# Weight operands prepared one step earlier, and two tiles placed elsewhere in memory, in a fused attention and two-MoE kernel

## The chip, the cores and the metric

The kernel runs on one core of a Trainium2 chip. The metric is device time in microseconds (us), the median of several executions. Before the change it was 1088.23 us over three runs (1085.76 to 1088.39).

## What is computed

Three layers follow each other. The first is linear attention with exponential features (4 batches, 8 heads, 576 positions); the second is a soft mixture of experts with 32 slots; the third, in which the change lies, is a dense mixture of 8 experts over 2304 tokens of width 512, hidden width 1024, with weights P that come from a gate by eight rounds of row and column normalisation:

```
logits = x @ w_gate
P = np.exp(logits - logits.max())
for _ in range(8):
    P /= P.sum(1, keepdims=True) + 1e-09
    P /= P.sum(0, keepdims=True) + 1e-09
    P *= N / E
for e in range(E):
    h = np.maximum(x @ w1[e], 0.0)
    out += P[:, e:e + 1] * (h @ w2[e])
```

All of it is float32 in and out.

## The kernel before

The last layer takes some 800 of the 1084 us. Its input x is the product of a coefficient matrix (2304 x 32) and the 32 slot outputs, so `x @ w1[e]` is made as a product of rank 32. Each float32 operand is split into two parts, high and low, and stacked, so that a single pass over 128 rows gives the exact product. For expert e, `make_stack` multiplies slot outputs with w1 (tile `ps`), VectorE (DVE) splits the result into the second half of the tile `st`, `spread_stack` spreads it over the partitions (matmuls `pr`, weights `rep`), and ScalarE (ACT) writes both halves of `st`. The coefficients stand in five tiles `ct0` to `ct4`; `ct0` to `ct3` hold two blocks of 256 tokens each, `ct4` one.

A block is 256 tokens of one expert; there are 9 to an expert, 72 in all. In a block, `first_layer` issues 8 matmuls `z<-ct,st` (stationary operand: 128 columns of `st`; moving operand: 256 columns of `ct`). `hidden` applies relu and forms the operands of a Strassen-Winograd product with seven products in place of eight: ACT writes each operand's high part (`hh_a` from z directly, `hh_s` from a sum s), DVE or GpSimd (POOL) the low part (`hl_a` on DVE, `hl_s` on POOL: four per block), DVE the sums s. `product(i, k)` then multiplies operand k of block i with the matching operand of w2: 4 chunks by 3 matmuls (high by high, high by low, low by high), 12 of them, into a sum named x, y or z. `take` adds the sum, times P, to the output tile `xo` on DVE. The order of the products k = 0 to 6 is a11, a12, s2, s1, s3, s4, a22, with the weight operands b11, b21, t2, t1, t3, b22, t4; t1 to t4 are differences or sums of quarters of w2.

The weight operands of the next expert are prepared while this one runs. `w_sum(e, n)` makes t1, t2, t3, t4 (n = 0 to 3) on POOL; t4 is made in the place of b21. `w_part(e, k)` makes operand k: ACT writes its high part (a CAST of 128x1024), then POOL its low part (a TENSOR_TENSOR of 128x1024). In the profile b11, b21 and b22 all read `w_b`, t1 to t4 read `w_t`, and a sum's line has `moe_w` or `t` as its output. They go into ten buffers in turn, so that operand k >= 3 of expert e+1 takes the place of operand k-3 of expert e.

The order of the work is written out by hand and kept on each engine. In the main loop, after each product (block `blk`, step `k`), one piece of `hidden` for the next block is issued, then what the tables `W_SUMS` and `W_PARTS` have under `(blk, k)`; a key of 9 stands for block 0 of the expert that is being prepared. `first_layer` of the next block is issued behind the product of k = 2, so between two first layers run the products s1, s3, s4, a22 of one block and a11, a12, s2 of the next. During expert 0, `SINK` also issues pieces of the gate's normalisation, mainly three at k = 1 and two at k = 5; these are small DVE instructions on P and on row and column sums (`rs`, `cs`).

Tiles are laid out one behind the other in pools. `rd_held` takes 16 bytes of a partition, rounded up to 32, and `gst`, the gate's tile, 32. So before the change `ct4` starts at byte 32032 (32 past a multiple of 256) and `st` at byte 190240 (also 32 past). `ct0` to `ct3` and `rep` start at multiples of 256. The `hh` and `hl` tiles stand 96 past a multiple of 256, the weight operands 32 past.

Of the kernel before, what the change touches and what calls it, by code (L numbers as in the profile page):

```python
# [8 lines left out]
F32R = mybir.dt.float32r  # L9
# [9 lines left out]
E, SPE, FF = 8, 4, 1024  # L19
# [34 lines left out]
def tile_kernel(ctx: ExitStack, tc: tile.TileContext, a):  # L54
# [3 lines left out]
    const = ctx.enter_context(tc.tile_pool(name="const", bufs=1, side="left"))  # L58
# [8 lines left out]
    def load_const(name, shape, pool=None, q=SP):  # L67
        t = (pool or const).tile(shape, F32, name=name, bufs=1)
        q.dma_start(out=t, in_=a[name])
        return t  # L70
# [9 lines left out]
    def w1_unit(name, e, n):  # L80
        return unit_t[name, e, n].rearrange("p (k f) -> p k f", k=2)
# [21 lines left out]
    def load_k(t):  # L103
        x = kp.tile([128, 512], F32, tag="kt", name=f"kt{t}")
        SP.dma_start(out=x, in_=a["kT"][t])
        kt_t[t] = x

    def load_v(i):
        x = kp.tile([128, 512], F32, tag="vt", name=f"vt{i}", bufs=3)
        SP.dma_start(out=x, in_=a["vb"][i])  # L110
        vt_t[i] = x
# [287 lines left out]
    load_k(1)  # L399
    load_v(0)  # L400
    load_k(2)
    ident = load_const("ident", [128, 128])
    ones = load_const("ones", [128, 128])
    sel_e = load_const("sel_e", [128, 4], kp)
# [113 lines left out]
    mp = mp_cm.__enter__()  # L518

    ct = [const.tile([128, 512], F32R, tag=f"x{i}", name=f"ct{i}", bufs=1) for i in range(4)]  # L520
    ct.append(const.tile([128, 256], F32R, name="ct4", bufs=1))
    rep = [const.tile([128, 4, 128], F32R, tag=f"x{4 + i}", name=f"rep{i}", bufs=1) for i in range(2)]
    for i in range(2):
        G.dma_start(out=rep[i], in_=a["rep"][:, i * 512:(i + 1) * 512].rearrange("p (g c) -> p g c", g=4))
# [99 lines left out]
    def w_sum(e, n):  # L624


        w = wsrc[e]
        if n == 0:
            G.tensor_tensor(out=w["t1"], in0=w["t3"], in1=w["b11"], op=ALU.subtract)
        elif n == 1:  # L630
            G.tensor_tensor(out=w["t2"], in0=w["t1"], in1=w["b22"], op=ALU.subtract)
        elif n == 2:
            G.tensor_tensor(out=w["t3"], in0=w["t3"], in1=w["b22"], op=ALU.subtract)
        else:
            G.tensor_tensor(out=w["t4"], in0=w["t4"], in1=w["t2"], op=ALU.add)

    def w_part(e, k):

        name = PRODUCTS[k][1]
        s = wsrc[e][name]  # L640
        n = (7 * e + k) % NW
        w = (cl1 if n < 4 else cl2).tile([128, 2, KH, 256], F32R, tag=f"wo{n}", name=f"w{e}_{name}", bufs=1)
        A.copy(out=w[:, 0], in_=s)
        G.tensor_tensor(out=w[:, 1], in0=s, in1=w[:, 0].bitcast(F32), op=ALU.subtract)
        wop[e, k] = w
        if k == 6:
            wsrc.pop(e)
            for n in range(2):
                unit_t.pop(("moe2_w2", e, n))
# [70 lines left out]
    cp = ctx.enter_context(tc.tile_pool(name="cp", bufs=1, side="right", reuse_waits="tile"))  # L720
    pz = ctx.enter_context(tc.tile_pool(name="pz", bufs=1, space=PSUM, reuse_waits="tile"))
    pm = ctx.enter_context(tc.tile_pool(name="pm", bufs=4, space=PSUM, reuse_waits="tile"))
    xo = cp.tile([128, NT, DM], F32, name="xo")
    P = cp.tile([128, NT, E], F32, name="P")

    def acc_tile(name):
        return pm.tile([128, 512], F32, tag="m", name=name)

    def z_tile(n, name):
        return pz.tile([128, 1024], F32, tag=f"z{n}", name=name)  # L730

    def make_stack(e):

        ps = z_tile(0, f"ps{e}")[:, 0:256]
        for kc in range(KC):
            w = w1_unit("moe2_w1", e, kc // 2)
            for g in range(4):
                PE.matmul(ps[32 * g:32 * g + 32, :], sot[:, kc, 0:NS], w[:, kc % 2, g * 256:(g + 1) * 256], start=kc == 0, stop=kc == KC - 1)
        for n in range(2):
            unit_t.pop(("moe2_w1", e, n))  # L740

        st = cp.tile([128, FF], F32R, tag="st", name=f"st{e}", bufs=1)
        hl = st[:, FF // 2:].rearrange("p (n f) -> p n f", n=2)
        V.tensor_copy(out=hl[:, 0, :], in_=ps)
        V.tensor_tensor(out=hl[:, 1, :], in0=ps, in1=hl[:, 0, :].bitcast(F32), op=ALU.subtract)
        return st
# [11 lines left out]
    def sinkhorn():  # L758
# [11 lines left out]
        yield  # L770
        Pf = P.rearrange("p t e -> p (t e)")
        V.tensor_copy(out=Pf, in_=pl[:, 0:NT * E])
# [11 lines left out]
        V.tensor_scalar_sub(Pf, Pf, gm)  # L784
        A.activation(out=P, in_=P, func=AF.Exp)
        yield
        for it in range(8):
            rs = cp.tile([128, NT, 1], F32, tag="rs", name=f"rs{it}")
            V.tensor_reduce(out=rs, in_=P, axis=AX.X, op=ALU.add)
            V.tensor_scalar_add(rs, rs, 1e-9)  # L790
            V.reciprocal(out=rs, in_=rs)
            yield
            V.tensor_tensor(out=P, in0=P, in1=rs.to_broadcast([128, NT, E]), op=ALU.mult)
            yield
            cs = cp.tile([128, 1, E], F32, tag="cs", name=f"cs{it}")
            csf = cs.rearrange("p o e -> p (o e)")
            V.tensor_reduce(out=csf, in_=P.rearrange("p t e -> p e t"), axis=AX.X, op=ALU.add)
            yield
# [4 lines left out]
            yield  # L803
            V.tensor_tensor(out=P, in0=P, in1=cs.to_broadcast([128, NT, E]), op=ALU.mult)
            yield
# [116 lines left out]
    sink = sinkhorn()  # L922
    next(sink)
    stacks = {0: make_stack(0)}
    for k in (4, 5, 6):
        w_part(0, k)
# [7 lines left out]
        pass  # L934
    load_munits(4)

    W_SUMS = {(3, 1): 0, (3, 6): 1, (5, 6): 2, (7, 6): 3}
    W_PARTS = {(2, 6): 0, (4, 6): 2, (6, 6): 1, (8, 1): 3, (8, 6): 4, (9, 0): 5, (9, 1): 6}
    SINK = {1: 3, 5: 2}
    making = iter(())  # L940
    for i, (e, blk) in enumerate(blocks):
# [3 lines left out]
        for k in range(7):  # L945
            product(i, k)
            take(i, k)
            if k == 0 and blk == NBLK - 1 and more:
                stacks[e + 1] = make_stack(e + 1)
            if k == 1 and blk == NBLK - 1 and more:  # L950
                spread_stack(stacks[e + 1], e + 1)
            if k == 2 and i + 1 < len(blocks):
                first_layer(i + 1, 1)
                first_layer(i + 1, 0)
                making = hidden(i + 1)
            next(making, None)
            if more and (blk, k) in W_SUMS:
                w_sum(e + 1, W_SUMS[blk, k])
            if more and (blk, k) in W_PARTS:
                w_part(e + 1, W_PARTS[blk, k])  # L960
            if e and (blk + 9, k) in W_PARTS:
                w_part(e, W_PARTS[blk + 9, k])
            if e == 0:
                for _ in range(SINK.get(k, 0) - (blk == 0 and k == 1)):
                    next(sink, None)
            if i == NBLK - 1 and k in (3, 4):
                scale_row(k - 3)
            if e == 1 and k in (0, 1) and blk + 1 < NBLK:
                scale_row(2 * (blk + 1) + k)
# [66 lines left out]
```

## Time and profile before

| | |
|---|---|
| median of three runs | 1088.23 us (1085.76 to 1088.39) |
| profiled execution, whole | 1086.3 us |
| its span, first to last instruction | 1084.1 us |
| TensorE matmul (PE) busy | 1052.2 us, 97% |
| TensorE weight load (PEld) busy | 982.0 us, 91% |
| VectorE (DVE) busy | 732.0 us, 68% |
| GpSimd (POOL) busy | 687.3 us, 63% |
| ScalarE (ACT) busy | 569.8 us, 53% |

Busy time of PE counts a matmul from its start to its end, and the ends overlap: a matmul over 256 columns shows about 0.28 us, while the next one starts 0.113 us later. So a wait of PE shows as a longer distance between starts before it shows as idle time, and distances between starts are the safer measure. Within the main loop every line of the profile is put down to one helper's line (L50); instructions are told apart by their tiles.

### The profile page before, as it was taken

How to read it: one execution, taken by the hardware profiler on the slowest of the kernel's cores; microseconds unless marked ns; L12 is line 12 of the kernel's file. 1: busy time of each engine (PE TensorE's matmuls, PEld its weight loads, DVE VectorE, ACT ScalarE, POOL GpSimd, SP SyncE). 2: the span in 40 equal slices, each digit the busy share in tenths (PEclk: the TensorE clock that was granted, in tenths of full speed). 3: DMA queues.
4: the chain of work that ended last, by engine and by line, in shares of the span. 5: the costliest groups of instructions: out<-in, count | busy, mean ns of one | idle time of the engine just before them, and what ended most of it. 6: DMA issues, size and time to landing. Idle time of an engine off the chain costs nothing.

```text
span 1084.1 us, 23152 instructions
## 1 busy us (share of the span) xinstructions
PE 1052.2 (97%) x9206; PEld 982.0 (91%) x9206; DVE 732.0 (68%) x1518; ACT 569.8 (53%) x1009; POOL 687.3 (63%) x442
## 2 busy tenths in 40 slices
PE   7999999999899999999999999999999999999998
PEld 5688788853899999999999999999999999999998
DVE  6878777850578767665766666576667666665765
ACT  5665544312556576654556454655555564545542
POOL 4776551107556777777777577767777775777443
PEclk9999999999899999999999999999999999999999
DMA  7772115379400130022003100300220031000111
GB/s 264 246 272 88 54 40 205 146 279 399 158 2 2 36 121 1 2 79 79 2 1 117 40 2 16 141 2 1 79 79 1 2 112 46 2 1 21 54 45 60
DMA packets 22571, 89.26 MB, mean 82 GB/s; under 512 B 2752, under 2 KB 5568, under 8 KB 14272
## 3 DMA queue, kind: packets, MB, share of 16 engines
q1 hardware_dynamic: 22176, 87.26, 22.2%
q8 instruction: 73, 1.20, 0.5%
q0 software_dynamic: 288, 0.52, 0.2%
q14 instruction: 34, 0.28, 0.1%
HBM read 83.05 MB, written 4.72 MB: 81 GB/s over the span
## 4 chain that ended last, share of the span: by engine, by line
PE 78%; POOL 11%; DVE 5%; issue 2%; DMA 2%; ACT 1%; SPq 0%; POOLq 0%; DVEq 0%; ACTq 0%
PE x L50 30%; PE y L50 14%; PE z L50 12%; PE num L271 6%; POOL hl_s L50 5%; POOL w_t L50 3%; PE kvacc L179 3%; POOL w_b L50 2%; PE ut L246 1%; PE ps L50 1%; DVE s L50 1%; PE kvp L218 1%; DMA moe_w<-in_moe_w 1%; PE pk L142 1%; PE ph L50 1%
## 5 line engine op out<-in xcount | busy, mean ns | idle before, releaser
L50 POOL TENSOR_TENSOR hl_s<-s,hh_s 128x512 fp32r<-128x512 f32 x288 | 367.5, 1298 | 230.1 <-ACT hh_s L50 214.0
L50 PE MATMUL x<-w_t,hh_s 128*128 128x256 f32 x1152 | 205.4, 278 | 3.9 <-DVE xo L50 2.7
L50 ACT ACTIVATE hh_s<-s 128x512 fp32r<-128x512 f32 x288 | 175.7, 629 | 53.0 <-DVE s L50 49.1
L50 PEld LDWEIGHTS x<-w_t,hh_s 128*128 128x128 f32 x1152 | 173.8, 188 | 5.3 <-issue 3.9
L50 DVE SCALAR_TENSOR_TENSOR xo<-x,P,xo 128x256 f32<-128x256 f32 x252 | 121.1, 481 | 75.3 <-PE x L50 75.3
L50 ACT ACTIVATE hh_a<-z 128x512 fp32r<-128x512 f32 x216 | 122.2, 600 | 90.1 <-DVE s L50 88.3
L50 ACT ACTIVATE r<-z 128x512 f32<-128x512 f32 x144 | 86.1, 598 | 156.6 <-PE z L50 156.2
L50 PE MATMUL x<-w_t,hl_s 128*128 128x256 f32 x576 | 159.7, 277 | 0.0
L50 DVE SCALAR_TENSOR_TENSOR s<-z,r 128x512 f32<-128x512 f32 x144 | 98.9, 687 | 86.7 <-ACT hh_a L50 82.2
L50 DVE SCALAR_TENSOR_TENSOR hl_a<-z,hh_a 128x512 fp32r<-128x512 f32 x216 | 147.4, 683 | 0.0
L50 DVE SCALAR_TENSOR_TENSOR s<-z,s 128x512 f32<-128x512 f32 x144 | 98.5, 684 | 19.4 <-POOL hl_s L50 17.9
L50 PE MATMUL x<-w_t,hh_a 128*128 128x256 f32 x576 | 104.2, 279 | 6.3 <-POOL w_t L50 4.9
L50 PEld LDWEIGHTS x<-w_t,hl_s 128*128 128x128 f32 x576 | 108.3, 188 | 0.0
L50 PE MATMUL y<-w_b,hh_s 128*128 128x256 f32 x576 | 103.8, 278 | 0.2 <-POOL w_b L50 0.2
L50 PE MATMUL x<-w_b,hh_a 128*128 128x256 f32 x576 | 103.1, 279 | 0.0
L50 PE MATMUL z<-w_b,hh_a 128*128 128x256 f32 x576 | 103.0, 279 | 0.0
L50 PE MATMUL y<-w_t,hh_s 128*128 128x256 f32 x576 | 102.9, 278 | 0.0
L50 PEld LDWEIGHTS x<-w_t,hh_a 128*128 128x128 f32 x576 | 87.5, 188 | 7.9 <-POOL w_t L50 6.2
L50 PEld LDWEIGHTS z<-w_b,hh_a 128*128 128x128 f32 x576 | 87.3, 189 | 2.9 <-issue 2.9
L50 PEld LDWEIGHTS y<-w_b,hh_s 128*128 128x128 f32 x576 | 87.5, 188 | 1.4 <-POOL w_b L50 1.3
L50 PEld LDWEIGHTS x<-w_b,hh_a 128*128 128x128 f32 x576 | 87.7, 190 | 0.0
L50 PEld LDWEIGHTS y<-w_t,hh_s 128*128 128x128 f32 x576 | 87.6, 188 | 0.0
(213 smaller groups left out, 2342.1 us busy)
## 6 DMA issues: line engine op xcount, KB each, us to landing
moe_w<-in_moe_w SPq DMA_DIRECT2D x64, 1024.0 KB, 6.9
vt<-in_vb SPq DMA_DIRECT2D x20, 256.0 KB, 3.7
kt<-in_kT SPq DMA_DIRECT2D x18, 256.0 KB, 3.1
qt<-in_qT SPq DMA_DIRECT2D x18, 256.0 KB, 2.8
out<-xo SPq DMA_DIRECT2D x18, 128.0 KB, 1.7
out<-xo SPq DMA_DIRECT2D x9, 256.0 KB, 2.0
rep<-in_rep POOLq DMA_DIRECT2D x2, 256.0 KB, 5.8
bd<-in_bd SPq DMA_DIRECT2D x1, 384.0 KB, 4.3
```

The costliest lines, as they stand in the source:

```text
L50: return lambda *args, **kwargs: self.tc.keep_in_program_order(make(*args, **kwargs))
L142: PE.matmul(o, hi[:, s], wbdh, start=True, stop=False)
L179: PE.matmul(acc[64 * j:64 * j + 64, p * 256:(p + 1) * 256], v[:, (2 * p + j) * D:(2 * p + j + 1) * D], phik[:, 2 * p + j].rearrange("p c f ...
L218: PE.matmul(ps[:, c * 192:(c + 1) * 192], kvt[:, p * 256 + c * 128:p * 256 + (c + 1) * 128], bd[:, p], start=True, stop=True)
L246: PE.transpose(ps[:, j * 128:(j + 1) * 128], uq_t[t][hh][:, j * 128:(j + 1) * 128], ident)
L271: PE.matmul(ps[r0:r1, j * XW:(j + 1) * XW], phiq[:, c, j * 128 + r0:j * 128 + r1], kvs_t[b][:, c, 4 * hh + j, :], start=c == 0, stop=c == 1,)
```

## The change

The diff has three parts. The tables ask for the last sum (t4, n = 3) at (7, 1) in place of (7, 6), for operand 3 at (8, 0) in place of (8, 1), operand 4 at (8, 1) in place of (8, 6), operand 5 at (8, 6) in place of (9, 0) and operand 6 at (9, 0) in place of (9, 1). `ct4` is allocated ahead of the constants, and starts at byte 16512 (128 past a multiple of 256). `st0` is allocated ahead of `gst`, and `st` starts at byte 190208 (a multiple of 256), with `gst` behind it at 194304. The other tiles of the first pool move up by 1024 bytes and keep their remainders; nothing else moves.

```
@@ -399,6 +399,7 @@
     load_k(2)
+    ct4 = const.tile([128, 256], F32R, name="ct4", bufs=1)
     ident = load_const("ident", [128, 128])
...
-    ct.append(const.tile([128, 256], F32R, name="ct4", bufs=1))
+    ct.append(ct4)
...
     P = cp.tile([128, NT, E], F32, name="P")
+    st0 = cp.tile([128, FF], F32R, tag="st", name="st0", bufs=1)
...
-        st = cp.tile([128, FF], F32R, tag="st", name=f"st{e}", bufs=1)
+        st = cp.tile([128, FF], F32R, tag="st", name=f"st{e}", bufs=1) if e else st0
...
-    W_SUMS = {(3, 1): 0, (3, 6): 1, (5, 6): 2, (7, 6): 3}
-    W_PARTS = {(2, 6): 0, (4, 6): 2, (6, 6): 1, (8, 1): 3, (8, 6): 4, (9, 0): 5, (9, 1): 6}
+    W_SUMS = {(3, 1): 0, (3, 6): 1, (5, 6): 2, (7, 1): 3}
+    W_PARTS = {(2, 6): 0, (4, 6): 2, (6, 6): 1, (8, 0): 3, (8, 1): 4, (8, 6): 5, (9, 0): 6}
```

The orders of PE, DVE and of the DMA queue are as before. ACT and POOL change at the seven places where one expert gives way to the next. On POOL, from the end of expert 1 into expert 2, before the change (block 17 is the last of expert 1, 18 and 19 the first two of expert 2; the names end in tile numbers, and the first number behind `hl_` and the operand is the block):

```order
L50 TENSOR_TENSOR hl_s3_17_5947<-s3_17_5929,hh_s3_17_5945 128x512
L50 TENSOR_TENSOR moe2_w2_2_1_4909<-moe2_w2_2_1_4909,t2_5061 128x4x256
L50 TENSOR_TENSOR w2_t1_6011<-moe2_w2_2_0_4907,w2_t1_6011 128x1024
L50 TENSOR_TENSOR hl_s1_18_6065<-s1_18_6042,hh_s1_18_6063 128x512
L50 TENSOR_TENSOR hl_s2_18_6084<-s2_18_6058,hh_s2_18_6082 128x512
L50 TENSOR_TENSOR hl_s4_18_6108<-s4_18_6088,hh_s4_18_6106 128x512
L50 TENSOR_TENSOR hl_s3_18_6127<-s3_18_6109,hh_s3_18_6125 128x512
L50 TENSOR_TENSOR w2_t3_6130<-moe2_w2_2_0_4907,w2_t3_6130 128x1024
L50 TENSOR_TENSOR w2_b22_6147<-moe2_w2_2_1_4909,w2_b22_6147 128x1024
L50 TENSOR_TENSOR w2_t4_6164<-moe2_w2_2_1_4909,w2_t4_6164 128x1024
L50 TENSOR_TENSOR hl_s1_19_6218<-s1_19_6195,hh_s1_19_6216 128x512
```

and the same stretch of POOL after it:

```order
L50 TENSOR_TENSOR hl_s3_17_5948<-s3_17_5930,hh_s3_17_5946 128x512
L50 TENSOR_TENSOR w2_t1_5985<-moe2_w2_2_0_4907,w2_t1_5985 128x1024
L50 TENSOR_TENSOR w2_t3_6014<-moe2_w2_2_0_4907,w2_t3_6014 128x1024
L50 TENSOR_TENSOR hl_s1_18_6068<-s1_18_6045,hh_s1_18_6066 128x512
L50 TENSOR_TENSOR hl_s2_18_6087<-s2_18_6061,hh_s2_18_6085 128x512
L50 TENSOR_TENSOR hl_s4_18_6111<-s4_18_6091,hh_s4_18_6109 128x512
L50 TENSOR_TENSOR hl_s3_18_6130<-s3_18_6112,hh_s3_18_6128 128x512
L50 TENSOR_TENSOR w2_b22_6133<-moe2_w2_2_1_4909,w2_b22_6133 128x1024
L50 TENSOR_TENSOR w2_t4_6150<-moe2_w2_2_1_4909,w2_t4_6150 128x1024
L50 TENSOR_TENSOR hl_s1_19_6218<-s1_19_6195,hh_s1_19_6216 128x512
```

Three long instructions stood between `hl_s3` of block 18 and `hl_s1` of block 19; now there are two, and t3 stands ahead of block 18's four `hl_s`. The sum t4 (the second line of the first piece) has left this stretch. It now follows `w_b` of operand 1, one block earlier, as POOL's order after the change shows in expert 0 (for expert 1; block 8 is the last of expert 0):

```order
L50 TENSOR_TENSOR w1_b21_4406<-moe2_w2_1_1_3300,w1_b21_4406 128x1024
L50 TENSOR_TENSOR moe2_w2_1_1_3300<-moe2_w2_1_1_3300,t1_3616 128x4x256
L50 TENSOR_TENSOR hl_s1_8_4498<-s1_8_4475,hh_s1_8_4496 128x512
L50 TENSOR_TENSOR hl_s2_8_4517<-s2_8_4491,hh_s2_8_4515 128x512
L50 TENSOR_TENSOR hl_s4_8_4541<-s4_8_4521,hh_s4_8_4539 128x512
L50 TENSOR_TENSOR hl_s3_8_4563<-s3_8_4542,hh_s3_8_4561 128x512
```

where before the change the sum followed the four:

```order
L50 TENSOR_TENSOR w1_b21_4406<-moe2_w2_1_1_3300,w1_b21_4406 128x1024
L50 TENSOR_TENSOR hl_s1_8_4497<-s1_8_4474,hh_s1_8_4495 128x512
L50 TENSOR_TENSOR hl_s2_8_4516<-s2_8_4490,hh_s2_8_4514 128x512
L50 TENSOR_TENSOR hl_s4_8_4540<-s4_8_4520,hh_s4_8_4538 128x512
L50 TENSOR_TENSOR hl_s3_8_4562<-s3_8_4541,hh_s3_8_4560 128x512
L50 TENSOR_TENSOR moe2_w2_1_1_3300<-moe2_w2_1_1_3300,t1_3616 128x4x256
```

So two long POOL instructions now stand directly one behind the other at the start of block 7's run. On ACT the CASTs move in the same way: that of t1 now stands ahead of the two CASTs of `st`, and two in place of three follow block 18's `hh_s3`.

## Rows read from the trace of the kernel before

**Rows 1.** Waits of PE from 300 us on: total us, times, longest.

```profile
PE x L50 <- POOL w_t L50: 4.9, 7, 0.7
PE x L50 <- DVE xo L50: 4.1, 8, 1.4
```

**Rows 2.** Timeline of PE: starts of first layers (start, us, instruction), experts 1 and 7.

```profile
391.25 1.11 PE L50 MATMUL z<-ct,st 128*128 128x256 f32 x8
403.56 1.11 PE L50 MATMUL z<-ct,st 128*128 128x256 f32 x8
...
978.23 1.11 PE L50 MATMUL z<-ct,st 128*128 128x256 f32 x8
988.71 1.10 PE L50 MATMUL z<-ct,st 128*128 128x256 f32 x8
1001.18 1.11 PE L50 MATMUL z<-ct,st 128*128 128x256 f32 x8
```

**Rows 3.** Timeline of PE in expert 2, blocks 0 and 1; in brackets idle before.

```profile
494.34 0.67 PE L50 MATMUL y<-w_b,hh_s 128*128 128x256 f32 x2
...
496.96 0.39 PE L50 MATMUL x<-w_t,hh_a 128*128 128x256 f32 x1 [0.70 <-POOL w_t L50]
...
501.66 0.47 PE L50 MATMUL x<-w_t,hh_s 128*128 128x256 f32 x2 [0.31 <-DVE xo L50]
```

**Rows 4.** Timeline of POOL in the same stretch.

```profile
480.65 2.41 POOL L50 TENSOR_TENSOR w_t<-moe_w,w_t 128x1024 fp32r<-128x1024 f32 x1 [2.20 <-ACT w_t L50]
...
492.13 2.43 POOL L50 TENSOR_TENSOR w_b<-moe_w,w_b 128x1024 fp32r<-128x1024 f32 x1
494.50 2.41 POOL L50 TENSOR_TENSOR w_t<-moe_w,w_t 128x1024 fp32r<-128x1024 f32 x1
496.84 2.57 POOL L50 TENSOR_TENSOR hl_s<-s,hh_s 128x512 fp32r<-128x512 f32 x2
```

**Rows 5.** Timeline of POOL in expert 2, block 3.

```profile
523.22 2.40 POOL L50 TENSOR_TENSOR w_b<-moe_w,w_b 128x1024 fp32r<-128x1024 f32 x1
525.70 2.41 POOL L50 TENSOR_TENSOR moe_w<-moe_w 128x1024 f32<-128x1024 f32 x1
528.06 2.57 POOL L50 TENSOR_TENSOR hl_s<-s,hh_s 128x512 fp32r<-128x512 f32 x2
```

**Rows 6.** Timelines in expert 0, blocks 3 and 7: POOL.

```profile
323.12 2.40 POOL L50 TENSOR_TENSOR moe_w<-moe_w 128x1024 f32<-128x1024 f32 x1
...
365.37 2.39 POOL L50 TENSOR_TENSOR w_b<-moe_w,w_b 128x1024 fp32r<-128x1024 f32 x1
```

**Rows 7.** The same: DVE.

```profile
320.95 2.25 DVE L50 TENSOR_TENSOR P<-P,cs 128x144 f32<-128x144 f32 x1
...
323.58 1.97 DVE L50 TENSOR_SCALAR rs<-rs 128x18 f32<-128x18 f32 x1
...
368.30 0.18 DVE L50 TENSOR_SCALAR rs<-rs 128x18 f32<-128x18 f32 x1
```

**Rows 8.** The same: PE in block 3.

```profile
328.18 0.50 PE L50 MATMUL x<-w_t,hh_a 128*128 128x256 f32 x2 [1.42 <-DVE xo L50]
```

**Rows 9.** Chain that ended last, expert 1, blocks 1 to 2 (start, us, what).

```profile
414.20 0.94 PE z L50 x8
415.14 1.38 PE y L50 x12
416.52 1.36 PE x L50 x12
```

**Rows 10.** The same chain, expert 1, blocks 7 to 8.

```profile
466.60 0.95 PE z L50 x8
467.56 1.41 PE y L50 x12
...
471.80 2.83 PE x L50 x24
...
478.05 0.93 PE pr L50 x8
```

## The prediction

> **What bounds the kernel now.** PE does: it is busy in nearly the whole of the last layer, so only what PE waits for, or what makes its matmuls follow each other less closely, is worth time. I read the waits of PE first. From 300 us on there are two of weight: seven for POOL's `w_t` and eight for DVE's `xo` [rows 1]. Seven is the number of changes from one expert to the next, so I looked at one there, on the timelines of PE and POOL, and then measured what such a change costs by the distance between first layers, one per block. In expert 7 the first interval is 978.23 to 988.71, 10.48 us, the second 988.71 to 1001.18, 12.47 [rows 2]: 1.99 us are lost there. In expert 1 the second interval is 403.56 - 391.25 = 12.31, a loss of 1.83 [rows 2]. There are seven such intervals, of 12.31 to 12.60 us, and their losses add up to 13.9. The view of waits shows less, 4.9 us and the seven smaller ones of the eight, since a matmul drawn 0.28 us long covers the start of each wait.
>
> The loss has three pieces in each change, here in expert 2. At 494.34 two matmuls of `w_b` take 0.67 where two usually take 0.39 (b22's low part comes late); at 496.96 PE has stood idle 0.70 for t4; at 501.66 it has stood idle 0.31 for an `xo` of DVE [rows 3]. POOL explains all three: it makes b22 from 492.13, t4 from 494.50 to 496.91, and only then the two `hl_s` of the next block, to 499.41 [rows 4]. DVE's sums wait for these `hl_s`, and the `xo` waits behind the sums.
>
> **The change, part by part.** *The tables* take one of three long POOL instructions out of this stretch and put it one place earlier, where POOL stands idle: it waited 2.20 us before the `w_t` at 480.65 [rows 4]. In the order after the change, b22 comes where t3 was, t4 where b22 was, and the `hl_s` where t4 was. So t4 would be done about 2.4 us sooner, near 494.5. PE asks for its low part near 496.1, or 495.8 once the wait for b22 is gone: 1.3 us to spare. The `hl_s` pair ends near 497.1 in place of 499.41. PE reaches the third wait some 1.2 us sooner (the first two waits are gone), and it was 0.6 to 0.7 late: 2.3 - 1.2 - 0.7 leaves 0.4 us to spare. That is little, but the trace has this very pattern in each expert at block 3: two long POOL instructions in contact, the `hl_s` pair right behind [rows 5], and PE does not wait there in experts 1 to 6 (the view has no eighth wait for `w_t`, and the eighth for `xo` is in expert 0) [rows 1]. So all seven losses go: **-13.9 us**. ACT's CAST of t1 now waits for the end of block 8's first product, with the two CASTs of `st` behind it; these wait for `pr`, at 478.05, while that product, the second half of the 24 from 471.80, ends at 474.63 [rows 10]; the CAST would be over near 475.8, so nothing is late. If it were, PE's first layer would wait, up to the 1.05 us of a CAST, seven times.
>
> *The sum t4* now follows operand 1's `w_b` directly, at the start of block 7. In experts 1 to 6 that is block 3's pattern again, free. In expert 0 it is not. There DVE runs the normalisation between its own work, and in block 3 it was held twice: a small product on P took 2.25 us, ending with POOL's `w_b`, and then a scalar addition on `rs` took 1.97, ending with POOL's sum at 325.52, where the same addition takes 0.18 in block 7 [rows 6, 7]. PE then stood idle 1.42 us [rows 8]; with the covered start that is 1.7. In block 7 today `w_b` runs 365.37 to 367.76 and nothing follows [rows 6], so the `rs` addition at 368.30 is free [rows 7]. After the change the sum runs from about 367.85 to 370.25, over that addition. I expect the second hold and PE's wait again: **+1.7 us**, once. Its bounds are 0 and 3.4. The Trainium skill, "SBUF — State Buffer", section "Who interferes with whom", says that an instruction of DVE with two SBUF inputs, or one in its two-port mode, is fully blocked by a GpSimd instruction that reads SBUF. By this rule, too, experts 1 to 7 are safe, for there each DVE instruction takes one input from PSUM.
>
> *The two places in memory* concern how closely matmuls follow each other. Behind a usual first layer, 12 matmuls take 1.36 us, 113 ns each; the 8 of the first layer take 0.94, 117.5 each, and the next 12 take 1.38 [rows 9]. Against 113 that is 0.03 and 0.02 us, 0.05 per block. Where `ct4` is the moving operand the 8 take 0.95, and the following products 1.41, 1.41, 1.41 and 2.83 for 24, until `make_stack` ends it [rows 10]: 0.04 + 3 x 0.05 + 0.11 = 0.30 per expert. No new pair of remainders is in the trace with 256 columns, so I bound it. At best all goes to 113: -64 x 0.05 - 8 x 0.30 = -5.6. At worst every first layer becomes like that of `ct4`, and the wide distance of 118 holds from one block to the next: 0.04 + 5 x 0.05 + 0.11 - 0.05 = 0.35 per block, +22 over 64 blocks. The nearest rows: with both operands at 32 it is 0.95, with the moving one at 0 it is 0.94 [rows 9, 10], and with the stationary one at 0 (`pr`) it is 0.93 [rows 10]; neither of the two last leaves a wide distance behind. Each step to 0 gains 1.3 to 2.5 ns a matmul. I take both to add, some 115 ns: 64 x 8 x 2.5 ns = 1.3 us, and for `ct4` 0.29 x 8 = 2.3: **-3.6 us**.
>
> A rule speaks against any gain here. The Trainium skill, "TensorE: Matmul & The Clock Gate", section "LDWEIGHTS (loading the stationary operand)", has the time of a weight load follow from its columns alone, and the section on the steps of a matmul gives the two operands ports of their own. By it the third term is nil. The rows have 12 matmuls of one shape at 1.36 and at 1.41, so something beside the columns counts; whether it is the address, no row shows alone.
>
> **The sum.** 1086.3 (span 1084.1 and 2.2 around it) - 13.9 + 1.7 - 3.6 = 1070.5. The median of the runs, 1088.23, lies 1.9 above the profiled execution and the lowest 0.5 below it; I add half of the 1.9 and forecast **1071.5**.
>
> **Rivals.** *Addresses don't matter*: the third term is nil, the wide distance has another cause, such as the phase that a wait leaves behind. For it: a wider distance is seen for a while behind some of the waits too. Against: `ct4` brings it each time, eight of eight. Time: 1086.3 - 12.2 + 1 = 1075.
>
> *Alignment hurts*: both operands at the same remainder may be what widens the distance, not the remainder 32. For it: with `ct4` both stood at 32, and that is the wide case; where they differ, it is less wide. The change makes both a multiple of 128 everywhere. Then every block runs at 118 until something breaks it: 1086.3 - 12.2 + 22 + 1 = 1097. It decides from the point where some 35 of 64 blocks are wide (35 x 0.35 = 12.2). Against it: aligned reads should need no more accesses than split ones, and each single step to 0 helped.
>
> *POOL stays late for the third wait*: the 0.4 us to spare are not there, and the wait of 0.6 to 0.7 stays seven times, +4.5: 1076. For it: the margin is the smallest of the three; against it: block 3.
>
> **Chances and range.** Forecast 0.61, addresses don't matter 0.20, third wait stays 0.09, alignment hurts 0.10. The first three are faster by far more than 0.3% (3.3 us, about what a measurement can tell). Alignment that hurts only in part could end within it, so faster 0.90, same 0.02, slower 0.08. Range 1065 to 1080: below, the best bound of the third term without the 1.7 (1086.3 - 13.9 - 5.6 = 1066.8, and a little); above, the third wait and no gain of addresses (1079.5).
>
> **What would show it.** Right: first layers 10.48 us apart at every change of expert, or 10.45; no wait of PE for `w_t`; a second wait of some 1.4 us for `xo`, in expert 0 near 370, with an `rs` addition of 2 us. For the third term: 8 first-layer matmuls in 0.92 or less, and 1.36 behind those of `ct4`. Wrong: 1.41 for 12 products in most blocks (alignment hurts), 0.94 and 1.41 as today (addresses don't matter), or a wait for `xo` in block 1 of each expert.

## The result, and the profile after the change

The changed kernel takes 1074.14 us (median of 4 runs, 1072.85 to 1077.0), the kernel before in the same comparison 1087.05 (4 runs, 1085.76 to 1088.39). The ratio is 0.9885, with a 95% interval of 0.9859 to 0.991. The forecast was 1071.5, with a range of 1065 to 1080. The profiled execution has a span of 1071.9 us, 12.2 less than before.

First what PE waits for from 300 us on (total us, times, longest), where [rows 1] had two kinds of wait:

```profile
PE x L50 <- DVE xo L50: 2.8, 2, 1.4
```

The seven waits for `w_t` are gone, and of the eight for `xo` the seven short ones. Two long ones are left, both in expert 0; before there was one.

The change of expert on POOL's timeline, and in its upper part block 7 of expert 0 (start, us, instruction; idle before it in brackets), to set against [rows 4, 6]:

```profile
365.41 2.40 POOL L50 TENSOR_TENSOR w_b<-moe_w,w_b 128x1024 fp32r<-128x1024 f32 x1
367.89 2.40 POOL L50 TENSOR_TENSOR moe_w<-moe_w,t 128x1024 f32<-128x1024 f32 x1
...
492.27 2.41 POOL L50 TENSOR_TENSOR w_t<-moe_w,w_t 128x1024 fp32r<-128x1024 f32 x1
494.63 2.55 POOL L50 TENSOR_TENSOR hl_s<-s,hh_s 128x512 fp32r<-128x512 f32 x2
```

PE's timeline at the same two places, against [rows 2, 3, 8]:

```profile
372.94 0.50 PE L50 MATMUL x<-w_t,hh_a 128*128 128x256 f32 x2 [1.38 <-DVE xo L50]
...
490.81 1.12 PE L50 MATMUL z<-ct,st 128*128 128x256 f32 x8
...
494.51 0.39 PE L50 MATMUL y<-w_b,hh_s 128*128 128x256 f32 x2
...
495.87 0.39 PE L50 MATMUL x<-w_t,hh_a 128*128 128x256 f32 x2
496.10 0.28 PE L50 MATMUL x<-w_t,hl_a 128*128 128x256 f32 x1
...
501.31 1.12 PE L50 MATMUL z<-ct,st 128*128 128x256 f32 x8
```

At the change of expert the low part of t4 ends at 492.27 + 2.41 = 494.68, and PE first needs it behind 495.87, 1.2 us later or more. The two matmuls of `w_b` at 494.51 take 0.39 in place of 0.67. The first layers are 501.31 - 490.81 = 10.50 us apart; before, the interval at a change was 12.31 to 12.60. In expert 0 the sum (`moe_w`) now lies directly behind `w_b`, and DVE's timeline shows what it covers; [rows 7] had this instruction at 0.18:

```profile
368.35 1.97 DVE L50 TENSOR_SCALAR rs<-rs 128x18 f32<-128x18 f32 x1
```

It ends at 370.32, within 0.03 of POOL's sum (367.89 + 2.40 = 370.29), and PE stands idle 1.38 at 372.94.

The chain that ended last (start, us, what) in blocks 1 to 2 and 7 to 8 of expert 1, against [rows 9, 10]:

```profile
403.86 0.96 PE z L50 x8
404.82 1.38 PE y L50 x12
...
466.90 0.94 PE z L50 x8
467.84 1.36 PE y L50 x12
...
471.93 2.72 PE x L50 x24
```

In a usual block the 8 matmuls of the first layer now take 0.96 where they took 0.94: `st` at remainder 0 has made them slower (e5_best and e3_sum_late below differ in that alone). Behind `ct4` the products take 1.36 and 2.72, where they took 1.41 and 2.83. From here on I call a distance of 113.4 ns close (12 matmuls in 1.36 us) and one of 117.8 ns wide (12 in 1.41). One stretch is wide that was close before: behind PE's wait in block 7 of expert 0, the products between the first two first layers of expert 1 take 1.41 each.

```profile
383.47 1.41 PE y L50 x12
384.88 1.41 PE x L50 x12
```

A measure for what follows. Profiled executions differ by some microseconds ahead of 290 us, whatever the kernel. The window from 280 to 290 us of the kernel before shows why (window, its length, busy time of PE, PEld, DVE, ACT and POOL, granted clock, DMA share, GB/s):

```profile
280.00:290.00 10.00, 8.47 (x56) 7.96 (x56) 7.17 (x14) 5.89 (x12) 5.04 (x4) 0.83 0.70 270
```

and the same window of the experiment e5_best:

```profile
280.00:290.00 10.00, 9.63 (x44) 9.11 (x45) 4.39 (x9) 4.28 (x8) 2.53 (x2) 0.50 0.66 249
```

The clock granted there was 0.83 in one and 0.50 in the other, that is, the 1.2 GHz level throughout. So I compare profiles by their rest: from the first layer that starts in block 0 of expert 0 (for block 1, near 289 us) to the end of the span. By it the change took 12.0 us.

| kernel | rest of the profiled execution, us | median of runs, us (runs) |
|---|---|---|
| before | 794.8 | 1087.05 (4) |
| the change | 782.8 | 1074.14 (4) |
| e1_tables | 782.6 | 1073.49 (4) |
| e2_tables_ct4 | 780.9 | 1071.64 (4) |
| e3_sum_late | 780.7 | 1072.54 (4) |
| e4_map_st | 785.9 | 1079.71 (1) |
| e5_best | 779.0 | 1070.02 (5) |
| e6_map_w | 802.5 | 1091.06 (1) |
| e7_pair | 781.4 | 1073.65 (4) |
| e8_tables_st | 782.6 | 1073.47 (4) |
| e9_32_0 | 777.3 | 1067.52 (4) |
| e10_pair_ct4 | 784.9 | 1072.89 (4) |

The kernel before had 1085.08 beside e1 to e4, 1087.55 beside e5 to e8 and 1086.9 beside e9 and e10. The 95% intervals of the ratios reach some 2 to 3.5 us to each side, so medians that lie 1 or 2 us apart don't tell two of these kernels apart. What follows on such differences rests on the rests and on distances on PE's timeline, in one profiled execution of each kernel.

### The profile page after: what moved, and what is told of

It is laid out like the page before. It is cut to its first block, busy times and chain, and to the rows that moved or that the text cites. A ratio compares the mean times of both kernels' runs of the same rounds, so it can differ in the third digit from the quotient of the medians.

```text
span 1071.9 us, 23152 instructions
## 1 busy us (share of the span) xinstructions
PE 1047.2 (98%) x9206; PEld 981.5 (92%) x9206; DVE 733.9 (68%) x1518; ACT 571.6 (53%) x1009; POOL 688.3 (64%) x442
## 4 chain that ended last, share of the span: by engine, by line
PE 90%; DVE 4%; POOL 2%; DMA 2%; issue 1%; ACT 1%; SPq 0%; DVEq 0%; POOLq 0%; ACTq 0%
PE x L50 36%; PE y L50 18%; PE z L50 15%; PE num L271 6%; PE kvacc L179 2%; PE ut L246 2%; PE ps L50 1%; PE kvp L218 1%; DMA moe_w<-in_moe_w 1%; PE ph L50 1%; PE pk L142 1%; PE pk L144 1%; POOL zs L197 1%; PE pq L142 1%; PE pq L143 1%
## 5 line engine op out<-in xcount | busy, mean ns | idle before, releaser
L50 PE MATMUL x<-w_t,hh_a 128*128 128x256 f32 x576 | 101.9, 277 | 2.8 <-DVE xo L50 2.8
L50 PE MATMUL y<-w_b,hh_s 128*128 128x256 f32 x576 | 101.5, 276 | 0.0
```

Source lines behind the costliest of these rows:

```text
L50: return lambda *args, **kwargs: self.tc.keep_in_program_order(make(*args, **kwargs))
```

## The experiments

**e1_tables: the tables alone.** Against the kernel before:

```
-    W_SUMS = {(3, 1): 0, (3, 6): 1, (5, 6): 2, (7, 6): 3}
-    W_PARTS = {(2, 6): 0, (4, 6): 2, (6, 6): 1, (8, 1): 3, (8, 6): 4, (9, 0): 5, (9, 1): 6}
+    W_SUMS = {(3, 1): 0, (3, 6): 1, (5, 6): 2, (7, 1): 3}
+    W_PARTS = {(2, 6): 0, (4, 6): 2, (6, 6): 1, (8, 0): 3, (8, 1): 4, (8, 6): 5, (9, 0): 6}
```

> The tables alone, with ct4 and st where they were before (both 32 past a multiple of 256). My theory (the whole gain is the tables, 13.9 us of PE's waits less one new wait of 1.7 in expert 0, and the two moves in memory cancel): a span of 1072, first layers of 0.94 us and 12 products of 1.41 behind those of ct4, as before the change; no wait of PE for w_t. Rival (the moves in memory carry part of the gain): a span of 1074 to 1077.

1073.49 us, ratio 0.9895 (0.9869 to 0.9921), and a rest of 782.6: the whole gain of the change. PE waits for no `w_t`, and twice for `xo`, in blocks 3 and 7 of expert 0. By the prediction's terms -13.9 + 1.7 = -12.2; measured 782.6 - 794.8 = -12.2. So the two moves in memory together are worth nothing, and what is left is why.

**e2_tables_ct4: the tables and ct4's place, st where it was.** As e1_tables, and

```
+    ct4 = const.tile([128, 256], F32R, name="ct4", bufs=1)
...
-    ct.append(const.tile([128, 256], F32R, name="ct4", bufs=1))
+    ct.append(ct4)
```

> The tables and ct4 moved, st left 32 past a multiple of 256. My theory (ct4's move gains 0.25 to 0.3 us in each expert, st's move loses about 0.025 us in each block): a span of 1069.5 to 1070, the 12 products behind the first layers of ct4 back at 1.36, and the first layers of the other blocks at 0.94 in place of the 0.96 of the changed kernel. Rival (addresses don't matter, the distance between matmuls follows from the phase that a wait leaves): a span of 1072, and 1.41 or 0.96 where the waits leave it so.

1071.64 us, and a rest of 780.9, 1.8 under e1_tables. The chain at block 8 of expert 1:

```profile
465.59 0.95 PE z L50 x8
466.55 1.38 PE y L50 x12
...
470.64 2.72 PE x L50 x24
```

The first layer on `ct4` is as slow as before (0.95), but the wide distance no longer lasts behind it. The distances between the starts, counted from the matmul ahead of a group to the group's last, give the same: over 113.4 each, block 8 before had 45 ns in the first layer and 5 x 52 behind it; now it has 45 + 20, and the product with `make_stack` in it takes some 42 more. From its first layer to the next, block 8 takes 0.20 us less in each of experts 1 to 6. In expert 7, where it runs to the end, it takes 0.56 less; in expert 0, where PE's wait falls into it, nothing. Together that is the 1.8. The change, which also moves `st`, has a rest 1.9 above this: `st` at remainder 0 costs what `ct4` gains.

**e3_sum_late: the change, with t4's sum at its old place.**

```
-    W_SUMS = {(3, 1): 0, (3, 6): 1, (5, 6): 2, (7, 1): 3}
+    W_SUMS = {(3, 1): 0, (3, 6): 1, (5, 6): 2, (7, 6): 3}
```

> The changed kernel with the sum t4 asked for at (7, 6) as before, the four operands kept one place earlier. My theory (POOL holds two DVE instructions in expert 0 when two long POOL instructions stand in contact, and the sum has no need to be early): the rs addition near 368 takes 0.18 us, PE waits for xo once in place of twice, 1.7 us less, a span near 1070.2, and no wait of PE at any change of expert. Rival (the sum's place is what frees POOL at the change of expert): waits of PE for w_t or xo come back, 0.3 to 2 us seven times, a span of 1074 or more.

1072.54 us; the median is 1.6 under the change's, which by itself could be noise, and the rest 2.1. The span is 1071.1; the expected 1070.2 is missed since the profiled execution was later ahead of the rest (the first layer for block 1 starts at 290.43, in the change at 289.16). PE waits for `xo` once; the first fence is the view of waits, the second DVE's timeline in block 7 of expert 0:

```profile
PE x L50 <- DVE xo L50: 1.4, 1, 1.4
```

```profile
369.66 0.18 DVE L50 TENSOR_SCALAR rs<-rs 128x18 f32<-128x18 f32 x1
```

Without a POOL instruction behind `w_b` the same addition takes 0.18 in place of 1.97, and the wait is gone. Of the 2.1 us, 1.76 are gained in block 8 of expert 0 and 0.33 in block 0 of expert 1, which the wait had left wide. No wait for `w_t` came back at the changes of expert: moving the sum was not needed there, and cost a wait.

**e4_map_st: st at another remainder in each expert.** The change, with a longer tile and a view that starts 32 bytes further in each expert, so `st` is at 32 e past a multiple of 256 in expert e (`ct0` to `ct3` at 0, `ct4` at 128).

```
-    st0 = cp.tile([128, FF], F32R, tag="st", name="st0", bufs=1)
+    st0 = cp.tile([128, FF + 64], F32R, tag="st", name="st0", bufs=1)
...
+        st = st[:, 8 * e:8 * e + FF]
```

> The changed kernel with a larger tile for st, in which expert e's stack starts 32 x e bytes past a multiple of 256, so that the stationary operand of the first layers has the remainders 0, 32, ... 224 in turn, while the moving one (ct0 to ct3) stays at 0. If the difference of the two remainders counts, modulo 128: the eight first-layer matmuls are 120 ns apart in experts 0 and 4, 117 in 1, 3, 5, 7 and 113 in 2 and 6. If it is the stationary operand's remainder of 32 alone that costs: 113 but for expert 1. If addresses don't matter: alike in all eight experts. The whole should end within 3 us of the changed kernel.

1079.71 us, a rest 3.1 above the change's. In nanoseconds over 113.4 each, a usual block's first layer and the 12 matmuls behind it, from the starts on PE's timeline: 51 + 28 at remainder 0, 32 + 20 at 32, 34 + 25 at 64, 43 + 49 at 96, 41 + 18 at 128, 46 + 33 at 160, 38 + 10 and 40 + 48 by turns at 192, 36 + 23 at 224. So places count, and none is better than 32 over all blocks of its expert; a rule by the difference of the two remainders does not fit the eight. At 96 all products kept the wide distance, block after block, and at 192 those of every second block. PE's chain at 96:

```profile
600.18 1.41 PE x L50 x12
601.59 0.95 PE z L50 x8
602.53 1.41 PE y L50 x12
```

These products have their own operands where they always were. Their distance was handed on to them.

**e5_best: the better part of each.** The kernel before, with the change's `W_PARTS` and `ct4`, but the old `W_SUMS` and the old place of `st`.

> W_PARTS and ct4 as in the change, W_SUMS and st as before. If the parts add up as they were measured so far, one wait of PE for xo (some 1.67 us) goes against the kernel with both tables and ct4 moved, which had 1071.64 us and a span of 1069.5: a span of 1067.8, a median of about 1070.0, some 4 us below the changed kernel, one xo wait in expert 0 (block 3), none in block 7, and first layers 10.46 us apart in blocks 0 to 7. Rival: what the wait gives back is taken again by the sum t4 at its old place, where it now has a neighbour: then a wait for w_t or xo shows at each change of expert and the median is 1071.6 or more.

1070.02 us over 5 runs, ratio 0.9856 (0.9833 to 0.9879); one wait for `xo`, none for `w_t`, as expected. The rest, 779.0, is 1.9 under e2_tables_ct4: 1.68 of it in block 8 of expert 0, where the wait was. It is 1.7 under e3_sum_late, which differs in `st` alone: 27 ns in each of 63 usual blocks are 1.7.

**e6_map_w: weight operands at other places.** The kernel of e5_best, with

```
-        w = (cl1 if n < 4 else cl2).tile([128, 2, KH, 256], F32R, tag=f"wo{n}", name=f"w{e}_{name}", bufs=1)
+        w = (cl1 if n < 4 else cl2).tile([128, 2 * KH * 256 + 56 * (n < 4)], F32R, tag=f"wo{n}", name=f"w{e}_{name}", bufs=1)
+        off = 8 * e if n < 4 else 0
+        w = w[:, off:off + 2 * KH * 256].rearrange("p (h k d) -> p h k d", h=2, k=KH)
```

> The kernel of e5_best, with the weight operands (the moving operand of the products) in the first four buffers at remainder 32 + 32 e in expert e, and in the other six at 160 always; their partner hh, hl stays at 96. Theory one, each pair of remainders has a spacing of its own, in the products as in the first layer: the products on buffers at 160 differ by 3 to 6 ns a matmul from those at 32 within expert 0, and those in the first four buffers change from expert to expert. Twelve matmuls then take 1.36 us for some and up to 1.44 us for others, and the span is up to 20 us over that of e5_best. Rival: products follow each other at 113.4 ns wherever their operands stand, and the first layer alone depends on places: then all seven products of all blocks take 1.36 us and the span is that of e5_best.

The longer tiles move each other, so the first four buffers start at 32, 0, 224 and 192, plus 32 e: more pairs than the expectation names. 1091.06 us (one run), a rest 23.5 above e5_best. The products' distance is as movable as the first layer's. From expert 5, on PE's chain:

```profile
790.25 1.36 PE x L50 x12
791.61 0.95 PE z L50 x8
792.56 1.41 PE y L50 x12
...
795.39 1.44 PE y L50 x12
...
801.06 1.41 PE x L50 x12
802.47 0.95 PE z L50 x8
```

The rival (places count in the first layer alone) falls. But theory one falls too, as it was put: the product s2 at 790.25 has its operand in a buffer at 160 and takes 1.36, and s2 of the next block, at 801.06 on the same buffer, takes 1.41. A pair has no distance of its own.

**e7_pair: the products' pair of places in the first layer.** The kernel of e5_best with `ct0` to `ct4` moved to 32 and `st` to 96 by padding (`rd_held` takes 256 bytes in place of 32, and `rep` moves to 32 too):

```
-        rd = const.tile([128, 4, 1], F32, name="rd_held") if held else qp.tile([128, 4, 1], F32, tag="rd", name=f"rd{t}_{hh}", bufs=2)
+        rd = const.tile([128, 64], F32, name="rd_held")[:, 0:4].unsqueeze(2) if held else qp.tile([128, 4, 1], F32, tag="rd", name=f"rd{t}_{hh}", bufs=2)
...
+    const.tile([128, 40], F32, name="pad0", bufs=1)
     ct4 = const.tile([128, 256], F32R, name="ct4", bufs=1)
...
+    const.tile([128, 32], F32, name="pad1", bufs=1)
...
+    cp.tile([128, 32], F32, name="pad2")
+    st0 = cp.tile([128, FF], F32R, tag="st", name="st0", bufs=1)
+    cp.tile([128, 40], F32, name="pad3")
...
-        st = cp.tile([128, FF], F32R, tag="st", name=f"st{e}", bufs=1)
+        st = cp.tile([128, FF], F32R, tag="st", name=f"st{e}", bufs=1) if e else st0
```

> The kernel of e5_best, with ct0 to ct4 at remainder 32 and st at 96, the pair at which the products (moving 32, stationary 96) follow each other at 113.4 ns. Theory one, the pair of remainders alone sets the spacing: the 8 matmuls of a first layer take 0.91 us, and the 12 behind them 1.36, 52 ns less per block than in the kernel with st left at 32: 3.3 us in 64 blocks, a span of about 1064.5 and a median near 1066.7. Rival: the remainder is not all, the first layer (rank 32 stacks, a new stationary operand for each matmul, the change of operand between the layers) has an excess of its own: then 0.94 us or more, a span of 1068 to 1071, and perhaps the wide spacing behind, as with ct4 and st both at 32.

1073.65 us, where theory one had 1066.7, and a rest 2.4 above e5_best, while the first layer is just what was hoped for. The chain in expert 6 shows both at once:

```profile
920.43 0.91 PE z L50 x8
921.34 1.36 PE y L50 x12
...
925.42 2.93 PE x L50 x24
928.35 1.41 PE z L50 x12
...
931.17 0.94 PE z L50 x8
```

From expert 1 to here every first layer takes 0.91 and every product away from `make_stack` 1.36. At 925.47 one matmul comes 0.1 us late (220 ns behind the one before it); from then to the end of the kernel, with the same instructions at the same places, a product takes 1.41 and a first layer 0.94, some 0.40 us per block. So the distance has two values, 113.4 and 117.8 ns, and with these places nothing brings it back from there to the end. In expert 0, where PE is disturbed in each block, it flips from block to block.

The same matmul comes late in every kernel here but e6_map_w, 174 to 220 ns behind the one before it; why, no run shows. What follows it differs. In the kernel before, the change, e3, e5, e8 and e9 the distance is close again within eight matmuls. In e1, e2 and e4 it stays wide until the next first layer and the product behind it bring it back, and in e7 and e10 to the end. The kernels e2_tables_ct4 and e5_best have all tiles at the same places and differ only in when the sum t4 is made, and the matmul comes almost equally late (183 and 186 ns behind the one before). The chain in e2_tables_ct4:

```profile
926.09 2.89 PE x L50 x24
928.98 1.41 PE z L50 x12
```

and in e5_best:

```profile
928.81 2.81 PE x L50 x24
931.61 1.36 PE z L50 x12
```

So places alone don't settle it.

**e8_tables_st: tables and st, ct4 where it was.** As e1_tables, with the change's two lines on `st0`.

> Both tables and st at remainder 0, ct4 left where it was (32). If the parts add up, st costs what the changed kernel lost against the tables with ct4 moved (1074.14 - 1071.64 = 2.5 us): a median of 1073.49 + 2.5 = 1076.0, first layers' 8 matmuls at 120 ns (48 to 51 ns over 8 times 113.4, 28 in the 12 behind). Block 8 (ct4 at 32, st at 0) is then at the spacing of ct at 32 and st at 0, which no run has shown. Rival, the parts do not add up: ct4 at 32 with st at 0 is close (nothing wide behind it), then the median is near 1074.

The parts do not add up. 1073.47 us and a rest of 782.6, the same as e1_tables: usual first layers have the 51 + 28 ns, +27 in each of 63, but `ct4` (32) with `st` (0) is close:

```profile
466.64 0.93 PE z L50 x8
467.56 1.36 PE y L50 x12
468.93 1.36 PE x L50 x12
```

Either move alone ends the wide distance behind `ct4`. The second to be made can't gain that again, and moving `st` also costs 1.7.

**e9_32_0: ct at 32, st at 0 in all blocks.** The kernel of e7_pair, with `pad2` of 72 words and without `pad3`.

> The kernel of e7_pair with st at remainder 0 (ct0 to ct4 at 32). In e8_tables_st block 8 had this pair: 8 matmuls 26 ns over 8 times 113.4, the 12 behind at 113, and it came out of a wider stretch closely. If the pair does this in all blocks, whatever came before, a block saves 52 - 26 = 26 ns against ct0 to ct3 at 0 and st at 32 (e5_best), 1.5 us in 56 blocks and some 0.04 us in each block 8: 1.8 us, a median of about 1068.2 and a span of 1066. Against e7_pair: no stretch at 118, so less spread between runs. Rival: what block 8 showed hangs on what ct0 to ct3 (at 0) left behind; then wide stretches as in e7_pair, a median of 1071 or more.

1067.52 us (1066.19 to 1069.16), ratio 0.9822 (0.9803 to 0.9841), a span of 1066.0: as expected, and the fastest kernel here. Its interval lies below the change's and overlaps that of e5_best; the rest is 1.7 under e5_best, 26 ns in each usual block. The chain in expert 6:

```profile
918.14 0.93 PE z L50 x8
919.07 1.36 PE y L50 x12
...
923.15 2.83 PE x L50 x24
925.98 1.36 PE z L50 x12
```

One matmul comes 0.1 us late here as well (in the 24 at 923.15), but it leaves no wide stretch behind. From expert 1 on no wide stretch outlasts the product it begins in. In expert 0, four first layers (of blocks 2, 3, 5 and 7) are entered at the wide distance, and each time it is close again after four or so matmuls of the product behind; in e7_pair three of these four (2, 5 and 7) keep it through all their products.

**e10_pair_ct4: e7_pair, with ct4 at 128.** `pad0` now stands behind `ct4`.

> The kernel of e7_pair with ct4 at remainder 128 (ct0 to ct3 at 32, st at 96). In e7_pair every block of experts 1 to 6 had 113 ns throughout until PE was late once, at block 4 of expert 6, and then 118 to the end of the kernel: the same instructions at the same places, so the spacing is kept from one matmul to the next until something sets it anew. If one first layer in nine with another pair sets it to the close spacing, as the first layers at (0, 32) and (128, 32) did, no wide stretch outlasts one expert: some 0.05 us per block saved in 55 blocks against e5_best, 2.8 us less 0.06 per expert: a median near 1067.7. Rival: ct4 at 128 with st at 96 sets it to wide, as st at 96 did with ct at 0 in e4_map_st: then most blocks are at 118, 0.40 us each, a median of 1085 or more.

1072.89 us (1068.22 to 1078.47), the widest spread of all, and both expectations are half right. The profiled execution is the slowest of the four (1078.47). In it the chain comes into `ct4`'s first layer at the wide distance three times; in expert 1 it leaves closely, in experts 6 and 7 it does not. Experts 1 and 6:

```profile
468.66 1.41 PE x L50 x12
470.08 0.94 PE z L50 x8
...
472.39 1.36 PE x L50 x12
...
954.56 1.41 PE x L50 x12
955.97 0.93 PE z L50 x8
...
958.32 1.41 PE x L50 x12
```

The pair (128, 96) doesn't set the distance; how it leaves depends on more than the two remainders.

## Why the prediction was right, and where not

**What bounds the kernel** was read rightly: PE, with two kinds of wait [rows 1], and losses that the distance between first layers measures and the view of waits does not.

**The tables, -13.9:** right in size and in mechanism. All seven losses are gone (intervals of 10.5 us), t4 is done at 494.68 (predicted near 494.5), the `hl_s` pair at 494.63 + 2.55 = 497.18 (predicted near 497.1), and no wait for `xo` is left at a change. e1_tables shows it with the places as they were: all seven intervals are 10.48 us. The rival of a third wait that stays is refuted.

**The sum, +1.7:** right. The hold is again 1.97 us, the wait 1.38 idle, and e5_best gains 1.68 there against e2_tables_ct4; e3_sum_late takes it away by taking the POOL instruction away, nothing else. The held instruction is a scalar addition on 18 columns: 0.18 without and 1.97 with a POOL instruction beside it. The Trainium skill, "SBUF — State Buffer", section "Who interferes with whom", names two SBUF inputs or the two-port mode as what lets GpSimd block a DVE instruction; the hold agrees with it, while no row shows in which mode an addition with one SBUF input runs.

**The two places, -3.6:** wrong; measured about 0. The step that failed is "Each step to 0 gains 1.3 to 2.5 ns a matmul. I take both to add, some 115 ns". It was read from three rows in three different surroundings, as if each remainder had a price. With `st` at 0 a usual first layer takes 120 ns a matmul, not 115, and with the 12 behind it 79 ns over 113.4 each in place of 52, 27 ns more. Where `ct4` is the moving operand there is a gain, but less than was forecast. Between the starts of first layers, the change against e1_tables, which has its tables alone, shows:

| | us |
|---|---|
| expert 0 | +0.20 |
| block 0 of expert 1, wide behind the wait | +0.36 |
| the other 55 usual blocks of experts 1 to 7 (27 ns each, less 0.2 for a wide stretch in expert 6 of e1_tables) | +1.25 |
| block 8 in experts 1 to 6 | -1.08 |
| block 8 in expert 7, to the end | -0.60 |
| together | +0.13 |

The forecast had -1.3 for the usual blocks and -2.3 for those of `ct4`. The rests say the same: -12.0 for the change, -12.2 for the tables.

**The rivals on places.** "Addresses don't matter" gave the right total (1075 against 1074.14) for a wrong reason: e4 and e6 move nothing but places and cost up to 23.5 us. "Alignment hurts" was right in sign for `st`, and wrong in size: the wide distance didn't last. The phase that the first of these rivals named as another cause is, with the places, the other half of it: e7_pair keeps the distance that a late matmul left, with no place changed, and e2_tables_ct4 and e5_best part behind the same late matmul with all tiles at the same places. The Trainium skill's rule that the prediction sets against any gain ("TensorE: Matmul & The Clock Gate", section "LDWEIGHTS (loading the stationary operand)") has the time of a weight load follow from its columns alone, and gives the right total as well. The rows decide against it as the whole account: with the same columns and a granted clock of 1.00 the matmuls of a first layer follow each other at 113.4 to 119.8 ns on average.

So the time came within 2.6 us because the tables, the largest term, and the sum carry it; the forecast's third term was no better than none. Luck made the miss smaller: the profiled execution was forecast at 1070.5 and took 1074.14, 3.6 more, the whole third term, and the 1 us added for the median hid a part of that. What stays open is the rule by which a pair of places hands on, closes or widens the distance; e10_pair_ct4 shows that it is no table of pairs.

## What to carry to other kernels

Where several long instructions of a helper engine meet at a boundary, move the one that can stand earlier into that engine's idle time, and check what the new neighbour blocks: here one moved sum held a tiny instruction of another engine for 1.97 us. Move one thing at a time; two moves that end the same loss don't add. A matmul's distance is a state, not a constant: look at it over whole stretches, and prefer places that brought it back after each disturbance seen (e9_32_0) to places that are perfect until one comes (e7_pair).

## What the hardware showed that I had not expected

In the products, matmuls of one shape (128 x 128 by 256 columns) with nothing to wait for keep one of two distances over whole stretches, 113.4 or 117.8 ns, with the granted clock at 1.00 (in every kernel here from 300 to 1050 us). In first layers, and where the places of the operands change, single ones come up to 128 ns apart. Which of the two it is depends on where both operands start in a partition's memory, in steps as small as 32 bytes (e4_map_st), and on what ran before. With (32, 96) it stayed close for some 540 us in e7_pair, until one matmul came 0.1 us late, and then wide for the last 148. A first layer costs 0 to 51 ns over its 8 x 113.4 by the pair of places, and at one and the same pair, (32, 96), 0 or 36 by the distance at which it is entered. The rests of the best and the worst places tried differ by 802.5 - 777.3 = 25 us, twice what the tables gained.
